# Three places for a group's transposes, and a residual added by VectorE behind the attention

## The chip, the cores and the metric

The kernel runs on one core of a Trainium2 chip. The metric is the device time of one execution in microseconds (us). TensorE (PE in the profile) does matmuls and writes PSUM; VectorE (DVE), ScalarE (ACT) and GpSimd (POOL) work on SBUF, the first two on PSUM as well; SyncE (SP) issues transfers, as POOL does for weights.

## The reference

Two branches over one normalised input, S = 2048 tokens of D = 640, H = 32 heads of 20, F = 1536:

```python
xn = _layernorm(x)
q, k, v = split(xn @ wqkv)                      # 32 heads of 20
# token s attends to s, s-2, ..., s-14 (W = 8, dilation 2), -1e9 where the index is negative
attn = softmax(einsum("bhsd,bhswd->bhsw", q, kg) * 20 ** -0.5)
s = einsum("bhsw,bhswd->bhsd", attn, vg) @ wo
g = silu(silu(xn @ w1) @ w2)
return x + s * g
```

All is float32. The kernel splits every matmul operand into a high and a low part and adds three products (high by high, low by high, high by low), so each product stands three times in PE's stream.

## The kernel before, in words

The tokens are worked on in four groups of 512 (`NG = 4`; two halves of the sequence by two parities), each as four tiles (`T = 4`) of 128 tokens. A group passes through two stages.

`qkv_phase` computes q, k and v in four quarters of eight heads. A quarter runs over five chunks (`DC`) of the 640 inputs and, in each, over the four tiles, three matmuls each (L706 to L708). Behind a quarter, ScalarE moves the sums out of PSUM (L490, L493, L496), SP issues copies that shift k and v by partitions (`halo`, L508), and VectorE gets the attention of the quarter: the scores (L531 product, L534 sum, L540 to L544), the softmax (L553 to L556) and the values (L563 product, L568 and L571 sums), which end in the tile `O`. VectorE falls behind PE, so the attention of a group goes on through the next stage and into the next group's.

`ffn_phase` runs over the twelve chunks of F. PE computes the w1 product of chunk f (L862 to L864) and then the w2 product of chunk f - 1 (L741, L743). ScalarE applies SiLU twice (L868 high part, L869 full), VectorE takes the low part (L870). The result, through SiLU, is the gate tile `G` (L901).

The attention's result must be turned before it meets `wo`. `o_chunk` does this for 128 columns of `O`: four transposes on PE into one of two PSUM banks `rot` (L474, in `split_t`), a copy by ScalarE (L478) and the low part by VectorE (L479). For groups 0 to 2 the five chunks are turned in the QKV stage of the next group, at places given by `O_AT` as (quarter, chunk). For the last group chunks 0 to 2 are turned in its own feed-forward stage (`OL_AT`), and chunks 3 and 4 together by `o_rest` (L589 transposes, L592 and L593 copies), two tiles at f = 11 and two at f = 12 (`REST_AT`).

`wo_phase` of group g stands behind the first w1 unit of group g + 1: five `wo` units, then VectorE multiplies the gate by each sum (L773), which also frees PE's accumulators for w2. Then it adds the residual: SP loads x into one of two tiles `XR` (L779), POOL adds (L780), SP stores (L782). An entry called "hold" keeps VectorE free for 3.4 us in the planned order. `wo_last` does the same for the last group at the end of the kernel, with VectorE adding the residual (L799, L801) and SP storing each part as it is done (L805).

Weights come through a ring of seven tiles `w`. In group 0 and in part in group 1 they are loaded raw by SP (L378), split by ScalarE (L406) and VectorE (L412), and the halves stored (L417); later they are loaded ready by POOL (L398). The raw loads of `wo` fall into group 1.

The order of instructions on each engine is made ahead of time. Each step is handed to `Weave.add` with its engine, an assumed duration, the keys that it reads and writes, and a priority. `Weave.order` plays these through and gives every engine a fixed order; PE keeps the order in which its steps were added. On the chip an engine works through its list and waits at an instruction until its inputs are ready, with everything behind it waiting too.

Of the kernel before, what the change touches and what calls it, by code (L numbers as in the profile page):

```python
# [14 lines left out]
P = 128  # L15
# [160 lines left out]
def local_attention_silu_ffn(ctx: ExitStack, tc: tile.TileContext, x, wqkv, wo, w1, w2, out):  # L176
# [52 lines left out]
    ACC = [psum.tile([P, TOK], F32, name=f"acc{i}") for i in range(6)]  # L229
    ROT = [psum.tile([P, TOK], F32, name=f"rot{i}") for i in range(2)]  # L230
    carry = [dram.tile([2, NQ, 2, T, CQ], F32, name=f"carry{par}") for par in range(2)]
    PRK = [("pr", k) for k in range(DC)]
    count = {"acc": 0, "rot": 0, "t": 0, "xr": 0}

# [101 lines left out]
    def raw_load(k):  # L336


        if k >= len(fresh):
            return  # L340
        i = fresh[k]
        u = units[i]
        n = width(i)
        if k < DC:
            r, kr = PR.rearrange("p t w m -> p (t w m)")[:, k * n:(k + 1) * n], [PRK[k]]
        elif k < early:
            s = (k - DC) % 6
            r, kr = (XR[s], [("xr", s)]) if s < 2 else (G[:, s - 2, :], [("g", s - 2, 0), ("g", s - 2, CA)])
            r = r[:, :n]
        else:  # L350
            s = k % 2
            r, kr = XR[s][:, :n], [("xr", s)]
        raws[i] = r, kr
        more = []
        if u[0] == "q":
            _, q, c = u
            cols, m, at = parts(i), 3, 0
            whole = wqkv[c * P:(c + 1) * P, :]
            src = whole.rearrange("p (s m) -> p s m", s=3)[:, :, q * CQ:(q + 1) * CQ]
            if i >= first_q:  # L360
                if q < NQ - 1:
                    odd, lies = cols[3], 3 * CQ
                else:
                    odd, lies, src, m, at = cols[0], 0, src[:, 1:], 2, cols[0][1]
                more.append((r[:, lies:lies + odd[1]], whole[:, odd[0]:odd[0] + odd[1]]))
            dst = r[:, at:at + m * CQ].rearrange("p (s m) -> p s m", s=m)
        elif u[0] == "w1":
            src = w1.rearrange("(c p) f -> p c f", p=P)[:, :, u[1] * P:(u[1] + 1) * P]
            dst = r.rearrange("p (c f) -> p c f", c=DC)
        else:  # L370
            m = wo if u[0] == "wo" else w2
            src, dst = m[u[1] * P:(u[1] + 1) * P, :], r
        if k in BY_ACT:
            add("ACT", 0.65, lambda: nc.scalar.dma_start(dst, src), [], kr, -1, nbytes=n * P * 4)
            return

        def go():
            nc.sync.dma_start(dst, src)  # L378
# [311 lines left out]
    def qkv_phase(g, i, io):  # L690
        for q in range(NQ):
            if g == 0 and q == 0:
                ps = first_quarter(i)
            else:
                ps = [bank() for t in range(T)]
                for c in range(DC):
                    wh, wl, kh, kl = w_next("q", q, c)
                    for t in range(T):
                        o, kp = ps[t]

                        n = wh.shape[-1]

                        def unit(c=c, t=t, o=o, wh=wh, wl=wl, n=n):
                            o = o[:, :n]
                            hi, lo = TH[i][:, c, tsl(t)], TL[i][:, c, tsl(t)]
                            nc.tensor.matmul(o, hi, wh, start=c == 0, stop=False)  # L706
                            nc.tensor.matmul(o, lo, wh, start=False, stop=False)  # L707
                            nc.tensor.matmul(o, hi, wl, start=False, stop=c == DC - 1)  # L708
# [50 lines left out]
    def wo_phase(g, i):  # L759
# [11 lines left out]
        for p, kp, ts, cs in tm_views(banks):  # L771
            n = (ts.stop - ts.start) * (cs.stop - cs.start)
            dve(n, lambda p=p, ts=ts, cs=cs: nc.vector.tensor_tensor(  # L773
                out=G[:, ts, cs], in0=p, in1=G[:, ts, cs], op=OP.mult), [kp], gkeys(ts, cs), 0)
        add("DVE", HOLD, lambda: None, [("g", t, CA) for t in range(T)], ["hold"], 0)
        for t in range(T):
            s = take("xr", 2)
# [3 lines left out]
                [("g", t, 0), ("g", t, CA)], [("xr", s)], 500, lock=True)  # L781
            dma(lambda t=t, xr=xr: nc.sync.dma_start(rows(og, g)[:, t, :], xr), [("xr", s)], [], P * D * 4, clock[0] + 20)  # L782

    def wo_last(g, i):

        banks = tm_banks()
# [4 lines left out]
        tk = t_keys(i, range(DC))  # L791
        xr = [XR[t] if t < 2 else XIN[:, t, :] for t in range(T)]
        kx = [("xr", t) if t < 2 else ("xin", t) for t in range(T)]
        for t in range(T):
            dma(lambda t=t: nc.sync.dma_start(xr[t], rows(xg, g)[:, t, :]), [], [kx[t]], P * D * 4, clock[0] - 20)

        def give(p, kp, t, cs):
            n = cs.stop - cs.start
            dve(n, lambda: nc.vector.tensor_tensor(out=G[:, t, cs], in0=p, in1=G[:, t, cs], op=OP.mult),  # L799
                [kp], [("g", t, cs.start)], 0)  # L800
            dve(n, lambda: nc.vector.tensor_tensor(out=xr[t][:, cs], in0=xr[t][:, cs], in1=G[:, t, cs], op=OP.add),  # L801
                [("g", t, cs.start)], [kx[t]], 0, lock=True)

        def leave(t, cs):
            dma(lambda: nc.sync.dma_start(rows(og, g)[:, t, cs], xr[t][:, cs]), [kx[t]], [], P * 4 * (cs.stop - cs.start), 0)  # L805

        def whole(t, cols):
            for k in range(3):
# [4 lines left out]
        A, B = slice(0, CA), slice(CA, D)  # L813
        for t in range(T - 1):
            pe(15 * TM, lambda t=t: whole(t, (0, 1)), tk + kw, [a[t][1], b[t // 2][1]])
            give(a[t][0][:, :CA], a[t][1], t, A)
            if t:
                for u in range(t // 2 * 2, t + 1):
                    give(b[t // 2][0][:, u % 2 * CB:(u % 2 + 1) * CB], b[t // 2][1], u, B)
                    leave(u, slice(0, D))  # L820
        t = T - 1
        pe(15 * mm(CA), lambda: whole(t, (0,)), tk + kw, [a[t][1]])
        give(a[t][0][:, :CA], a[t][1], t, A)
        leave(t, A)

        def rest():
# [4 lines left out]
        pe(15 * mm(CB), rest, tk + kw, [klast])  # L831
        give(lastb[:, :CB], klast, t, B)
        leave(t, B)

    def ffn_phase(g, i, ix, io):
        nxt = g + 1 if g + 1 < NG else None
        ps = prev = None
        for f in range(FC + 1):
# [15 lines left out]
            if f < FC:  # L854
# [1 line left out]
                h, kp = rot()  # L856
                s = f % 2

                def first(wh=wh, wl=wl, h=h):
                    for c in range(DC):  # L860
                        cs = tsl(c)
                        nc.tensor.matmul(h, wh[:, cs], TH[i][:, c, :], start=c == 0, stop=False)  # L862
                        nc.tensor.matmul(h, wh[:, cs], TL[i][:, c, :], start=False, stop=False)  # L863
                        nc.tensor.matmul(h, wl[:, cs], TH[i][:, c, :], start=False, stop=c == DC - 1)  # L864
                pe(15 * mm(TOK), first, t_keys(i, range(DC)) + [kh, kl], [kp])
# [77 lines left out]
```

## Time and profile before

| | |
|---|---|
| three runs | 639.21, 639.41, 638.80 us; median 639.21 |
| the profiled execution | 639.21 us, its span 637.4 us |
| granted TensorE clock | 0.999 |
| busy: PE / DVE / ACT / POOL | 630.3 / 536.9 / 211.3 / 122.5 us |
| HBM read, written | 109.55 MB, 34.16 MB |

Rows of a timeline give start and length in us from the start of the span, the engine (a q behind it is its queue: issues and waits), the source line, the operation, the output tile and the inputs, the shape, and in brackets how long the engine had been idle and who ended that. Matmuls overlap, so the distance from one start to the next is what one costs in a full stream, not its length. Lines of groups give count, total and mean. Lines of waits give who waited, for whom, the total in us, how often, and the longest.

### The profile page before, as it was taken

The numbers are of one execution on the slowest core, as the hardware profiler recorded it, in microseconds if no ns is written. First come the engines' busy times: TensorE is split into PE (matmuls) and PEld (weight loads), VectorE is DVE, ScalarE is ACT, GpSimd is POOL, SyncE is SP. The second block draws the span as 40 slices with busy tenths as digits, with TensorE's granted clock in tenths as the row PEclk, the third lists the DMA queues.
The fourth block names the chain that finished last, engine by engine and source line by source line (L and its number), as shares of the span: only waits on it lengthen the run. The fifth ranks groups of instructions, "written<-read, shape, count | busy, mean of one in ns | idle before, by whom it ended". The sixth has DMA issues, their size and how long they took to land.

```text
span 637.4 us, 9082 instructions
## 1 busy us (share of the span) xinstructions
PE 630.3 (99%) x3495; PEld 569.1 (89%) x3495; DVE 536.9 (84%) x539; ACT 211.3 (33%) x439; POOL 122.5 (19%) x168
## 2 busy tenths in 40 slices
PE   7999999999999999999999999999999999999997
PEld 6888899998889989999888999999988999899997
DVE  7699899999989799999969998998405997999844
ACT  5436453443435013142422402324313231131420
POOL 4500000001110133111222125212122213311100
PEclk9999999999999999999999999999999999999999
DMA  9999999876998999657699988865679999966522
GB/s 282 302 316 297 325 392 407 321 215 218 294 300 257 349 323 295 205 176 219 194 244 234 323 241 298 276 192 164 177 198 261 244 328 275 299 214 198 174 83 82
DMA packets 77499, 162.45 MB, mean 255 GB/s; under 512 B 9248, under 2 KB 38912, under 8 KB 77456
## 3 DMA queue, kind: packets, MB, share of 16 engines
q0 software_dynamic: 26672, 82.58, 44.1%
q1 hardware_dynamic: 50240, 78.88, 39.5%
q8 instruction: 27, 0.44, 0.3%
q10 hardware_dynamic: 544, 0.41, 0.2%
q14 instruction: 16, 0.13, 0.1%
HBM read 109.55 MB, written 34.16 MB: 225 GB/s over the span
## 4 chain that ended last, share of the span: by engine, by line
PE 92%; DVE 4%; DMA 3%; issue 1%; ACT 0%; DVEq 0%; ACTq 0%
PE acc L741 20%; PE acc L743 14%; PE acc L706 10%; PE acc L707 10%; PE acc L708 10%; PE rot L864 8%; PE rot L863 8%; PE rot L862 8%; DMA xr<-in_A_wo_dram 2%; PE rot L474 2%; PE acc L649 2%; DVE w L412 1%; DVE st L614 1%; DMA xin<-in_A_x_dram 0%; DVE gate L773 0%
## 5 line engine op out<-in xcount | busy, mean ns | idle before, releaser
L706 PE MATMUL acc<-w,th 128*128 128x512 f32 (+2 forms) x300 | 114.4, 381 | 0.0
L741 PE MATMUL acc<-w,sh 128*128 128x384 f32 x384 | 113.7, 335 | 0.0
L707 PE MATMUL acc<-w,tl 128*128 128x512 f32 (+2 forms) x300 | 113.1, 377 | 0.0
L708 PE MATMUL acc<-w,th 128*128 128x512 f32 (+2 forms) x300 | 112.9, 376 | 0.0
L743 PE MATMUL acc<-w,sh 128*128 128x256 f32 x384 | 107.2, 279 | 0.1
L531 DVE TENSOR_TENSOR pr<-q,kv 128x2560 f32<-128x2560 f32 x32 | 90.3, 2823 | 10.5 <-DMA kv<-kv 10.4
L862 PE MATMUL rot<-th,w 128*128 128x512 f32 x240 | 95.4, 398 | 0.0
L864 PE MATMUL rot<-th,w 128*128 128x512 f32 x240 | 94.1, 392 | 0.0
L863 PE MATMUL rot<-tl,w 128*128 128x512 f32 x240 | 93.9, 391 | 0.0
L563 DVE TENSOR_TENSOR pr<-e,kv 128x2560 f32<-128x2560 f32 x32 | 90.3, 2823 | 0.7
L534 DVE TENSOR_REDUCE l<-pr 128x128 f32<-128x2560 f32 x32 | 90.0, 2814 | 0.3
L398 POOL DMA_DIRECT2D w<-half_q x52 | 37.3, 717 | 239.3 <-DVE pr L568 93.2
L568 DVE TENSOR_TENSOR pr<-pr 128x1280 f32<-128x1280 f32 x64 | 79.1, 1235 | 1.1
L398 POOL DMA_DIRECT2D w<-half_w x72 | 38.7, 537 | 189.5 <-PE acc L743 84.5
L743 PEld LDWEIGHTS acc<-w,sh 128*128 128x128 f32 x384 | 72.3, 188 | 2.1 <-DVE gate L773 0.4
L741 PEld LDWEIGHTS acc<-w,sh 128*128 128x128 f32 x384 | 72.1, 188 | 1.7
L868 ACT ACTIVATE sh<-rot 128x512 fp32r<-128x512 f32 x48 | 28.7, 598 | 129.8 <-PE rot L864 129.7
L708 PEld LDWEIGHTS acc<-w,th 128*128 128x128 f32 x300 | 56.3, 188 | 9.0
L706 PEld LDWEIGHTS acc<-w,th 128*128 128x128 f32 x300 | 56.3, 188 | 8.6
L707 PEld LDWEIGHTS acc<-w,tl 128*128 128x128 f32 x300 | 56.4, 188 | 8.5
L741 PE MATMUL acc<-w,sl 128*128 128x384 f32 x192 | 57.8, 333 | 0.0
L864 PEld LDWEIGHTS rot<-th,w 128*128 128x128 f32 x240 | 45.0, 188 | 9.9
(93 smaller groups left out, 982.9 us busy)
## 6 DMA issues: line engine op xcount, KB each, us to landing
w<-half_w POOLq DMA_DIRECT2D x72, 640.0 KB, 5.4
w<-half_q POOLq DMA_DIRECT2D x39, 512.0 KB, 4.1
half_w<-w SPq DMA_DIRECT2D x24, 640.0 KB
w<-half_wo POOLq DMA_DIRECT2D x15, 640.0 KB, 8.4
kv<-kv SPq DMA_DIRECT2D x16, 560.0 KB
kv<-kv SPq DMA_DIRECT2D x16, 420.0 KB
gate<-in_B_w_dram SPq DMA_DIRECT2D x16, 320.0 KB
w<-half_q POOLq DMA_DIRECT2D x13, 384.0 KB, 5.4
```

The lines of the kernel that those rows point to most:

```text
L531: dve(2560, lambda t=t: nc.vector.tensor_tensor(out=PR, in0=win(qq[:, t:t + 2, :], W, 0), in1=win(kv[:, 0, t:t + 2, :], W, CQ), op=OP.mult ...
L534: dve(2560, lambda t=t: nc.vector.tensor_reduce(out=l[:, t:t + 2].rearrange("p t w h -> p (t w h)"), in_=PR.rearrange("p t w (h d) -> p (t ...
L563: dve(2560, lambda t=t, v=v: nc.vector.tensor_tensor(out=PR.rearrange("p t w (h d) -> p t (w h) d", d=DH), in0=e[:, t:t + 2].rearrange("p ...
L568: dve(2 * n * CQ, lambda n=n: nc.vector.tensor_tensor(out=PR[:, :, 0:n, :], in0=PR[:, :, 0:n, :], in1=PR[:, :, n:2 * n, :], op=OP.add), [] ...
L706: nc.tensor.matmul(o, hi, wh, start=c == 0, stop=False)
L707: nc.tensor.matmul(o, lo, wh, start=False, stop=False)
L708: nc.tensor.matmul(o, hi, wl, start=False, stop=c == DC - 1)
L741: nc.tensor.matmul(a[t][0][:, :CA], st, w[:, :CA], start=first, stop=last)
L743: nc.tensor.matmul(b[t // 2][0][:, h * CB:(h + 1) * CB], st, w[:, CA:], start=first and h == 0, stop=last, skip_group_check=True)
L862: nc.tensor.matmul(h, wh[:, cs], TH[i][:, c, :], start=c == 0, stop=False)
L863: nc.tensor.matmul(h, wh[:, cs], TL[i][:, c, :], start=False, stop=False)
L864: nc.tensor.matmul(h, wl[:, cs], TH[i][:, c, :], start=False, stop=c == DC - 1)
```

## The change

It does three things. The five chunks of `O` of groups 0 to 2 are turned at three places of the next group's QKV stage, each behind a whole quarter: chunks 0 and 1 behind quarter 1, chunks 2 and 3 behind quarter 2, chunk 4 behind quarter 3. The residual of group 2, whose gate is finished in the last group's feed-forward stage, is no longer added by POOL there, and the hold is not planned; `wo_rest` has VectorE add it when the last group's attention is done, with two of the four x tiles in `XR` and two in the tile `PR`, which the attention then no longer needs. The last group's second `o_rest` moves from f = 12 into the last w1 unit, between its twelfth and thirteenth matmul. The last group's own residual uses the four tiles of `XIN`, and its steps carry finer keys.

```diff
-    O_AT = {(1, 1): 0, (1, 4): 1, (2, 3): 2, (3, 1): 3, (3, 3): 4}
+    O_AT = {(1, 4): (0, 1), (2, 4): (2, 3), (3, 4): (4,)}
-    REST_AT = {11: (0, 1), 12: (2, 3)}
+    REST_AT = {11: (0, 1)}
...
                     if g and (q, c) in O_AT:
-                        o_chunk(g - 1, O_AT[q, c], io)
+                        for k in O_AT[q, c]:
+                            o_chunk(g - 1, k, io)
...
@@ wo_phase, behind the products by the gate
+        if g == NG - 2:
+            for t in range(T):
+                xr, kx = (XR[t], [("xr", t)]) if t < 2 else (PRV[:, (t - 2) * D:(t - 1) * D], PRK)
+                rest.append((t, xr, kx))
+                if t < 2:
+                    dma(lambda t=t, xr=xr: nc.sync.dma_start(xr, rows(xg, g)[:, t, :]), [], kx, P * D * 4, clock[0] + 5)
+            return
         add("DVE", HOLD, lambda: None, [("g", t, CA) for t in range(T)], ["hold"], 0)
...
+    def wo_rest(g):
+        done = [("o", NQ - 1, t) for t in (0, 2)]
+        for t, xr, kx in rest:
+            if t >= 2:
+                dma(lambda t=t, xr=xr: nc.sync.dma_start(xr, rows(xg, g)[:, t, :]), done, [(kx[0], t)] if t > 2 else kx,
+                    P * D * 4, clock[0])
+        for t, xr, kx in rest:
+            kx = [(kx[0], t)] if t > 2 else kx
+            dve(D, lambda t=t, xr=xr: nc.vector.tensor_tensor(out=xr, in0=xr, in1=G[:, t, :], op=OP.add),
+                done + gkeys(slice(t, t + 1), slice(0, CA)) + gkeys(slice(t, t + 1), slice(CA, D)), kx, 600, lock=True)
+            dma(lambda t=t, xr=xr: nc.sync.dma_start(rows(og, g)[:, t, :], xr), kx, [], P * D * 4, clock[0] + 5)
...
@@ wo_last
-        xr = [XR[t] if t < 2 else XIN[:, t, :] for t in range(T)]
+        xr = [XIN[:, t, :] for t in range(T)]
...
@@ ffn_phase, the w1 unit
+                if nxt is None and f == FC - 1:
+                    pe(12 * mm(TOK), lambda first=first: first(range(4)), t_keys(i, range(DC)) + [kh, kl], [kp])
+                    o_rest(g, (2, 3), io)
+                    wo_rest(g - 1)
+                    pe(3 * mm(TOK), lambda first=first: first(range(4, DC)), t_keys(i, range(DC)) + [kh, kl], [kp])
+                else:
+                    pe(15 * mm(TOK), first, t_keys(i, range(DC)) + [kh, kl], [kp])
```

More of the change, by code (lines that the diff above doesn't have):

```diff
@@ L790, in wo_last @@
         kw = [k for w in ws for k in w[2:]]
[L791 to L793 removed]
+        tk = lambda t: t_keys(i, range(DC), [t])
+        xr = [XIN[:, t, :] for t in range(T)]
+        A, B = slice(0, CA), slice(CA, D)
+        kx = lambda t, *cs: [("xin", t)] + [("xin", t, c.start) for c in cs]
         for t in range(T):
[L795 removed]
+            dma(lambda t=t: nc.sync.dma_start(xr[t], rows(xg, g)[:, t, :]), [], kx(t, A, B), P * D * 4, clock[0] - 20)
         def give(p, kp, t, cs):
@@ L801, in give, with leave @@
             dve(n, lambda: nc.vector.tensor_tensor(out=xr[t][:, cs], in0=xr[t][:, cs], in1=G[:, t, cs], op=OP.add),
-                [("g", t, cs.start)], [kx[t]], 0, lock=True)
-        def leave(t, cs):
-            dma(lambda: nc.sync.dma_start(rows(og, g)[:, t, cs], xr[t][:, cs]), [kx[t]], [], P * 4 * (cs.stop - cs.start), 0)
+                [("g", t, cs.start)], kx(t, cs)[1:], 0, lock=True)
+        def leave(t, *cs):
+            at = slice(cs[0].start, cs[-1].stop)
+            dma(lambda: nc.sync.dma_start(rows(og, g)[:, t, at], xr[t][:, at]), kx(t, *cs)[1:], [],
+                P * 4 * (at.stop - at.start), 0)
         def whole(t, cols):
@@ L857, in ffn_phase, with first @@
                 s = f % 2
-                def first(wh=wh, wl=wl, h=h):
-                    for c in range(DC):
+                def first(cs=range(DC), wh=wh, wl=wl, h=h):
+                    for c in cs:
                         cs = tsl(c)
```

16 lines of the change are left out of this document (8 added, 8 removed).

## The prediction

> **What bounds the kernel now.** I read the page first: busy shares, then the chain that ended last.
>
> ```profile
> PE 630.3 (99%) x3495; PEld 569.1 (89%) x3495; DVE 536.9 (84%) x539; ACT 211.3 (33%) x439; POOL 122.5 (19%) x168
> ...
> PE 92%; DVE 4%; DMA 3%; issue 1%; ACT 0%; DVEq 0%; ACTq 0%
> ```
>
> TensorE (PE) is busy for 630.3 of 637.4 us and makes up 92% of the chain. A busy share can hide stalls, so next came the view of who waited for whom, for PE's rows and its weight loads (total us, times, longest).
>
> ```profile
> PE rot L628 <- DVE xin L619: 1.6, 3, 0.8
> PE rot L602 <- POOL ident masks.py:199: 1.4, 1, 1.4
> PE acc L649 <- DVE tl L636: 0.3, 1, 0.3
> ...
> PEld acc L743 <- DVE gate L773: 0.4, 1, 0.4
> ```
>
> The first three lie in the first quarter, at the start of the program, which the change leaves alone. The last is the only stall of the matmul stream behind it. So the change can gain on the path only what it takes out of PE's own stream, plus that 0.4 us, and it can lose by any new wait of PE. 0.2% of the time, about what a measurement of this kernel can tell from no change, is 1.28 us.
>
> **Part 1, transposes in three places instead of five.** In groups 1 to 3 PE still turns five chunks of O, with the same 60 transposes. The edit removes two breaks of the matmul stream in each group. Cost of a break, from PE's timeline (start, length) and the row of that line (min/median/max ns):
>
> ```profile
> 166.55 0.39 PE L708 MATMUL acc<-w,th 128*128 128x512 f32 x1
> 166.78 0.60 PE L474 MATMUL rot<-ident,o 128*128 128x128 f32 x4
> 167.13 0.49 PE L706 MATMUL acc<-w,th 128*128 128x512 f32 x1
> 167.46 0.39 PE L707 MATMUL acc<-w,tl 128*128 128x512 f32 x1
> ...
> L474 PE MATMUL rot<-ident,o x72: 270/272/273, 166.8 to 597.4; 128*128 128x128 f32 x72
> ```
>
> From the transposes' start to the second matmul behind them are 0.68 us; one matmul's spacing (166.55 to 166.78) is 0.23, so four transposes cost the stream 0.45 us. Four starts fit into 0.60 - 0.27 = 0.33 us, so the spacing is 0.11 and four of them are 0.44. Being a break of its own costs therefore only about 0.02 us, and 2 x 3 merged breaks give 6 x 0.02 = 0.1 us. Bounds, since no row shows eight transposes in a row: 0 if the second four wait for their bank as they do now, 6 x 0.45 = 2.7 if they vanished in the pipeline. I take 0.1, which the spacing of rows gives.
>
> Moving them shifts data dependencies too. Chunk 3 is turned two weight chunks earlier than now, behind quarter 2. It needs the O of quarter 3 of the group before. In group 1, where VectorE is fullest, its timeline has the last write of it here, and ScalarE's last eviction of quarter 2, which follows that quarter's matmuls, stands below it:
>
> ```profile
> 183.76 0.49 DVE L571 TENSOR_TENSOR o<-pr 128x320 f32<-128x320 f32 x1
> ```
> ```profile
> 190.24 0.44 ACT L490 ACTIVATE kv<-acc 128x320 f32<-128x320 f32 x1
> ```
>
> O is there 6 us before the turn: no wait.
>
> **Part 2, group 1, where VectorE's order changes.** The written order of the changed kernel puts the score reduction L534 ahead of the last `wo` weight's low half (L412), where now it is behind. The rows of VectorE, and of PE where it stalls:
>
> ```profile
> 217.58 0.83 DVE L412 TENSOR_TENSOR w<-xr,w 128x640 fp32r<-128x640 f32 x1 [3.93 <-ACT w L406]
> 218.32 2.81 DVE L534 TENSOR_REDUCE l<-pr 128x128 f32<-128x2560 f32 x1
> 221.17 2.83 DVE L563 TENSOR_TENSOR pr<-e,kv 128x2560 f32<-128x2560 f32 x1
> 223.91 3.14 DVE L773 TENSOR_TENSOR gate<-acc,gate 128x384 f32<-128x384 f32 x6
> ```
> ```profile
> 226.66 0.33 PE L741 MATMUL acc<-w,sh 128*128 128x384 f32 x1
> 227.11 0.39 PE L743 MATMUL acc<-w,sh 128*128 128x256 f32 x1
> ```
>
> VectorE idles 3.93 us for that weight and then has L534, L563 and the six L773 that free PE's accumulators. 227.11 - 226.66 is 0.45 where such a pair is 0.17 apart, and the following step is also 0.1 longer: 0.38 us lost. With L534 in the 3.93 us hole, L563 and L773 come 2.8 us earlier and the loss goes: -0.38.
>
> The same weight can become the next wait. PE first needs its low half at 218.89, and VectorE ends it at 218.41. Its raw load stands in SP's queue behind the halo copies of quarter 3, and those wait for ScalarE's last eviction L490. In the new order chunk 4's eviction L478 stands ahead of that L490:
>
> ```profile
> 167.41 0.60 ACT L478 ACTIVATE th<-rot 128x512 fp32r<-128x512 f32 x1 [0.51 <-PE rot L474]
> ...
> 201.59 0.44 ACT L490 ACTIVATE kv<-acc 128x320 f32<-128x320 f32 x1
> ...
> 216.81 0.74 ACT L406 ACTIVATE w<-xr 128x640 fp32r<-128x640 f32 x1 [10.68 <-DMA xr<-in_A_wo_dram]
> ```
> ```profile
> 202.05 4.50 SPq L508 DMA_DIRECT2D kv<-kv  x4
> ...
> 207.41 0.36 SPq L378 DMA_DIRECT2D xr<-in_A_wo_dram  x1
> ```
> ```profile
> 201.39 0.39 PE L862 MATMUL rot<-th,w 128*128 128x512 f32 x1
> ...
> 218.89 0.33 PE L741 MATMUL acc<-w,th 128*128 128x384 f32 x1
> ```
>
> The quarter's stream ends at 201.39 in either order, so chunk 4 is turned from 201.39 - 0.45 = 200.9; L478 follows 0.63 us behind the start of a turn (166.78 to 167.41) and takes up to 0.60, so L490 starts at 202.1 instead of 201.59. Halo copies, raw load (207.41) and L412 move by the same 0.5 us if the transfer does: end at 218.9 against a need at 218.86. Loss 0.05; between 0 (the transfer hides the shift) and 0.5 (the transfer, 9.4 us from 207.41 to 216.81, is longer by 0.5 as well).
>
> **Part 3, the other residual in the last group.** In group 3 four POOL adds leave, VectorE's planned hold goes, and behind the attention VectorE gets four adds of 640 columns, SP two loads into `pr` (the other two, into `xr`, come early) and four stores. One row of the waits of VectorE between 534 and 637, and its timeline:
>
> ```profile
> DVE sl L870 <- ACT sf L869: 7.6, 6, 4.0
> ```
> ```profile
> 550.53 4.09 DVE L568 TENSOR_TENSOR pr<-pr 128x1280 f32<-128x1280 f32 x2
> ...
> 602.59 0.69 DVE L870 TENSOR_TENSOR sl<-sf,sh 128x512 fp32r<-128x512 f32 x1 [1.32 <-ACT sf L869]
> 603.20 0.48 DVE L571 TENSOR_TENSOR o<-pr 128x320 f32<-128x320 f32 x1
> 603.72 2.83 DVE L563 TENSOR_TENSOR pr<-e,kv 128x2560 f32<-128x2560 f32 x1
> ...
> 607.06 2.34 DVE L568 TENSOR_TENSOR pr<-pr 128x1280 f32<-128x1280 f32 x2
> ```
>
> In the new order the last L571, which completes O, stands right behind the L870 of 602.59. So 0.5 + 2.8 + 2.3 = 5.6 us of work must come ahead of it. There are 7.6 us of waits, the longest the hold's, and 4.09 - 2.34 = 1.7 us that L568 lost beside a POOL add: 9.3 us of room. O is then complete at 603.7. PE turns its last half inside the last w1 unit, behind 12 of 15 matmuls:
>
> ```profile
> 607.34 0.39 PE L864 MATMUL rot<-th,w 128*128 128x512 f32 x1
> ...
> 611.70 0.60 PE L589 MATMUL rot<-ident,o 128*128 128x128 f32 x4
> ...
> 612.74 0.34 PE L741 MATMUL acc<-w,sl 128*128 128x384 f32 x1
> ```
>
> That is at 607.6, 3.9 us later than O. The turn itself moves (from 611.70) and adds nothing. What is queued behind the new adds on VectorE is the split of both halves of O and the last L870, for which PE's matmul of 612.74 waits. The two adds out of `xr` (0.83 each, as L412) end at 605.4; the two out of `pr` wait for loads issued from 603.8 on:
>
> ```profile
> 539.56 1.58 SPq L779 DMA_DIRECT2D xr<-in_A_x_dram  x2
> ```
> ```profile
> 545.45 1.59 POOL L780 TENSOR_TENSOR xr<-xr,gate 128x640 f32<-128x640 f32 x1
> ```
>
> The first of two loads of this size, issued at 539.56, was in use by POOL at 545.45: it took at most 5.9 us, so 609.7 here, and the second, 0.8 us (half of 1.58) behind it, is there when the first add is done. Two adds, the second split and L870 (1.6 + 0.6 + 0.6) then end at 612.5, 0.2 us before the need. Cost 0, with that cover. Behind the matmuls the chain is unchanged: last eviction, add, store.
>
> **Sum.** The profiled execution is 639.21 us (span 637.4 and 1.8 around it), which is also the median. -0.1 - 0.38 + 0.05 = -0.43: 638.8, a span of 637.0. With the bounds of these terms it is 638.3 to 639.3, and the three runs scatter by 0.6.
>
> **Rivals.** (a) Slower: the loads into `pr` land late, VectorE holds L870 and PE stalls. For it: the load of 207.41 took 9.4 us in a busy stretch (216.81), and stores and weight loads run beside these too. Against: the rows around 540. It decides from 6.1 us of landing on (609.9); at 9.4 us PE loses 3.3: 642.1. At 7.9 us it passes 0.2%. (b) Slower: the last `wo` weight is late. Its load waits for the slot of the last w1 unit, which now ends 0.45 us later, beside 6 transfers of 320 KB.
>
> ```profile
> 608.71 0.53 POOL L398 DMA_DIRECT2D w<-half_wo  x1 [3.34 <-PE rot L864]
> ```
> ```profile
> w<-half_wo POOLq DMA_DIRECT2D x15, 640.0 KB, 8.4
> ```
> ```profile
> 616.94 0.34 PE L741 MATMUL acc<-w,th 128*128 128x384 f32 x1
> ```
>
> PE needs it at 616.94. The median of 8.4 us behind 609.2 gives 617.6, a loss of 0.7 (639.5); with another 2 us of contention it is 641.5. Against: the median is that of busier stretches, and this load made 616.94 without a stall. The Trainium skill ("DMA: Bandwidth & Descriptors", Queues, rings and completion order) says that a DMA engine serves its queues in turn, packet by packet; by that the weights would share with the stores and not stand behind all of them. No run here shows it for this pair yet. The skill also has a rule against the change ("SBUF — State Buffer", SBUF: two separate sides): VectorE can lock the port over which POOL writes its descriptors. By it the issue at 608.71 would slip by up to two adds, 1.7 us. The L398 rows do not show it: 0.53 us at 608.71, beside a running L568. (c) Faster: merged transposes cost almost nothing, 2.7 instead of 0.1 us: 636.2. Against: spacing 0.11 within four. (d) Faster: VectorE, not PE, sets the end, and the 5.6 us of work done sooner show: 633.2. Against: PE's list of waits has no such row. (e) The `wo` weight of group 1 stalls by the full 0.5: 639.2, still within 0.2%.
>
> **How the numbers follow.** Forecast 638.8 with 0.72, (e) 0.06, (a) 0.09, (b) 0.05, (c) 0.06, (d) 0.02. Within 0.2% are the forecast and (e), 0.78; slower (a) and (b), 0.14; faster (c) and (d), 0.08. 638.0 to 640.4 holds the forecast with the scatter of the runs, (e), and the mild ends of (a) and (b).
>
> **What would show it.** Right: PE's waits lose L743 <- L773 and gain nothing; eight transposes take about 0.89 us of stream; VectorE's last L571 lies near 603, and L870 still ends before PE's sl matmuls. Wrong: PE or its weight loads waiting at L741 of the fifth `wo` unit in group 1 (near 218.8), at L741 <- L870 near 612.7, or at the fifth `wo` weight near 617.

## The result, and the profile after

The changed kernel takes 642.74 us (median of 15 runs, 638.40 to 644.41) against 638.91 for the kernel before (15 runs, 638.70 to 640.68): 1.0042 times the time of before, with a 95% interval of 1.0026 to 1.0057. It is slower by 2.7 us by the ratio, and it scatters: the fastest run is below every run of before, the slowest 6 us above that. The mean granted clock tells the runs apart: seven runs between 638.40 and 641.19 have 0.999 or 1.000, and all eight from 642.74 up have 0.995 to 0.997. The traces shown below have the clock at half in stretches of 3.41 us; one such stretch takes 3.41 x 0.5 = 1.7 us of 640 from the mean clock, or 0.0027, so a run at 0.997 had one and a run at 0.995 two.

The profiled execution of the changed kernel took 643.34 us, its span is 641.5 and its clock 0.995. Source lines are one to four higher than in the kernel before around here (L406, L412, L741, L743, L773 are now L407, L413, L743, L745, L775). First the view of who waited for whom, PE's rows.

```profile
PE rot L629 <- DVE xin L620: 2.0, 3, 1.1
PE acc L743 <- ACT w L407: 1.5, 1, 1.5
PE rot L603 <- POOL ident masks.py:199: 1.4, 1, 1.4
PE acc L743 <- DVE w L413: 0.3, 1, 0.3
```

The stall by the gated multiply is gone, as forecast. Two waits are new, both for the fifth `wo` unit in group 1: PE waits for the high half of the weight (L407), then for the low half (L413). This is the first place that the prediction named as what would prove it wrong. PE's timeline there (start, length, line; in brackets the idle time and who ended it):

```profile
219.42 0.28 PE L745 MATMUL acc<-w,tl 128*128 128x256 f32 x1
221.18 0.45 PE L743 MATMUL acc<-w,th 128*128 128x384 f32 x1 [1.48 <-ACT w L407]
221.46 0.28 PE L745 MATMUL acc<-w,th 128*128 128x256 f32 x1
222.03 0.45 PE L743 MATMUL acc<-w,th 128*128 128x384 f32 x1 [0.30 <-DVE w L413]
...
222.78 0.53 PE L743 MATMUL acc<-w,th 128*128 128x384 f32 x1
223.10 0.41 PE L745 MATMUL acc<-w,th 128*128 128x256 f32 x1
...
225.99 0.38 PE L743 MATMUL acc<-w,th 128*128 128x384 f32 x1
```

A step of the full stream is 0.17 behind an L743 and 0.12 behind an L745. From 219.42 to 221.18 are 1.76 us, so 1.64 are lost; from 221.46 to 222.03 another 0.46. Then comes a second loss that is no wait: from 222.78 to 225.99 twelve matmuls take 3.21 us where six pairs take 1.71, with PE never idle. The windows view says why (columns: busy time of PE, its weight loads, VectorE, ScalarE, GpSimd, then granted clock, DMA share, GB/s):

```profile
218.00:221.50 3.50, 2.02 (x14) 1.74 (x13) 0.34 (x1) 0.74 (x1) 0.00 (x0) 1.00 1.06 408
221.50:226.00 4.50, 4.20 (x19) 3.97 (x18) 4.50 (x5) 0.00 (x0) 1.06 (x2) 0.63 0.89 297
226.00:232.00 6.00, 6.00 (x34) 5.41 (x34) 2.23 (x5) 1.09 (x2) 2.67 (x3) 1.00 0.76 274
```

The clock is at half behind the wait, for 3.41 us from 222.64 on. With 0.2 us at the edges of that stretch the place costs 1.64 + 0.46 + 1.50 + 0.23 = 3.8 us.

Why the weight came late, from the timelines of SP's queue, ScalarE and VectorE:

```profile
203.48 4.26 SPq L509 DMA_DIRECT2D kv<-kv  x4
...
208.31 0.36 SPq L379 DMA_DIRECT2D xr<-in_A_wo_dram  x1
```
```profile
202.53 0.60 ACT L479 ACTIVATE th<-rot 128x512 fp32r<-128x512 f32 x1 [0.41 <-PE rot L475]
203.03 0.43 ACT L491 ACTIVATE kv<-acc 128x320 f32<-128x320 f32 x1
...
220.38 0.74 ACT L407 ACTIVATE w<-xr 128x640 fp32r<-128x640 f32 x1 [12.85 <-DMA xr<-in_A_wo_dram]
```
```profile
221.16 0.83 DVE L413 TENSOR_TENSOR w<-xr,w 128x640 fp32r<-128x640 f32 x1 [4.22 <-ACT w L407]
```

This execution's PE is 0.93 us behind that of before at this point (1.15 from the start-up, less 0.22 gained by merged turns). So the load's issue, 208.31, is 207.38 in the time of before (with those 0.93 us taken off), against 207.41: not late, although the last eviction (202.10 against 201.59) and the halo copies (202.55 against 202.05) did move by the 0.5 us that was forecast. What is longer is the time of the transfer, 12.1 us from 208.31 until ScalarE can use it, against 9.4.

The first QKV matmul of groups 1, 2 and 3, in the kernel before and then in the changed one, cuts the difference of the two spans, 641.5 - 637.4 = 4.1 us, into parts:

```profile
147.69 0.40 PE L706 MATMUL acc<-w,th 128*128 128x512 f32 x1
...
303.92 0.40 PE L706 MATMUL acc<-w,th 128*128 128x512 f32 x1
...
459.74 0.40 PE L706 MATMUL acc<-w,th 128*128 128x512 f32 x1
```
```profile
148.84 0.40 PE L707 MATMUL acc<-w,th 128*128 128x512 f32 x1
...
308.34 0.40 PE L707 MATMUL acc<-w,th 128*128 128x512 f32 x1
...
463.95 0.40 PE L707 MATMUL acc<-w,th 128*128 128x512 f32 x1
```

Start-up +1.15, group 1 159.50 against 156.23 or +3.27, group 2 155.61 against 155.82 or -0.21, the rest -0.1. Group 1 is 3.8 of late weight, less the 0.4 of the old stall and the 0.2 of merged turns.

The start-up lies ahead of everything that the change touches, and with it goes a clock at half as well. PE's own windows (busy time of PE, granted clock, DMA share, GB/s) show the two stretches of this execution, and the window ahead of the second:

```profile
7.60:11.01 3.41, 3.41 (x12) 0.50 1.08 337
...
219.22:222.64 3.42, 1.64 (x10) 1.00 0.89 345
222.64:226.05 3.41, 3.41 (x15) 0.50 1.00 323
```

The profiled execution of the kernel before has no such stretch at its start. So 1.15 of the 4.1 us between these two profiles is not the work of the change. The mean clock of a run without a trace tells that a stretch was lost, not where: of 35 runs of the kernel before on the chip of the first experiments, four have 0.994 to 0.997 too, and take 640.49 to 642.30 us.

### The profile page after: what moved, and what is told of

The parts are those of the page before. It is cut to its first block, busy times and chain, and to the rows that moved or that the text cites. A ratio compares the mean times of both kernels' runs of the same rounds, so it can differ in the third digit from the quotient of the medians.

```text
span 641.5 us, 9077 instructions
## 1 busy us (share of the span) xinstructions
PE 632.7 (99%) x3495; PEld 572.1 (89%) x3495; DVE 537.5 (84%) x543; ACT 210.2 (33%) x439; POOL 117.7 (18%) x164
## 4 chain that ended last, share of the span: by engine, by line
PE 93%; DVE 3%; DMA 2%; issue 1%; ACT 0%; DVEq 0%; ACTq 0%
PE acc L743 21%; PE acc L745 14%; PE acc L709 9%; PE acc L707 9%; PE acc L708 9%; PE rot L890 8%; PE rot L889 8%; PE rot L888 8%; PE rot L475 2%; DMA xr<-in_A_wo_dram 2%; PE acc L650 2%; DVE w L413 1%; DMA xin<-in_A_x_dram 1%; DVE l L535 0%; DVE st L615 0%
## 5 line engine op out<-in xcount | busy, mean ns | idle before, releaser
L743 PE MATMUL acc<-w,sh 128*128 128x384 f32 x384 | 113.6, 335 | 0.0
L745 PE MATMUL acc<-w,sh 128*128 128x256 f32 x384 | 107.1, 279 | 0.0
L535 DVE TENSOR_REDUCE l<-pr 128x128 f32<-128x2560 f32 x32 | 90.1, 2815 | 0.4
L569 DVE TENSOR_TENSOR pr<-pr 128x1280 f32<-128x1280 f32 x64 | 76.0, 1188 | 1.0
L745 PEld LDWEIGHTS acc<-w,sh 128*128 128x128 f32 x384 | 72.3, 188 | 1.6
L743 PEld LDWEIGHTS acc<-w,sh 128*128 128x128 f32 x384 | 72.1, 188 | 1.7
L743 PE MATMUL acc<-w,sl 128*128 128x384 f32 x192 | 57.9, 333 | 0.0
L491 ACT ACTIVATE kv<-acc 128x320 f32<-128x320 f32 x64 | 28.3, 442 | 84.8 <-PE acc L709 82.2
```

What stands on the lines that cost most here:

```text
L535: dve(2560, lambda t=t: nc.vector.tensor_reduce(out=l[:, t:t + 2].rearrange("p t w h -> p (t w h)"), in_=PR.rearrange("p t w (h d) -> p (t ...
L743: nc.tensor.matmul(a[t][0][:, :CA], st, w[:, :CA], start=first, stop=last)
L745: nc.tensor.matmul(b[t // 2][0][:, h * CB:(h + 1) * CB], st, w[:, CA:], start=first and h == 0, stop=last, skip_group_check=True)
```

## Experiments

Theory: the late raw load of the last `wo` unit in group 1, with the fall of the clock behind it, is the whole loss, and it follows from where the chunks are turned. Rivals: the residual in the last group costs it; or the long runs are a matter of the chip and not of the kernel. Times beside each other below come from the same chip.

**The two halves of the change, and two repairs** (before: 639.08 us).

Places only, on the kernel before:

```diff
-    O_AT = {(1, 1): 0, (1, 4): 1, (2, 3): 2, (3, 1): 3, (3, 3): 4}
+    O_AT = {(1, 4): (0, 1), (2, 4): (2, 3), (3, 4): (4,)}
```

> Only the three places for the transposes; the residual stays with POOL and the hold stays. Theory A (the last wo weight's raw load comes late in group 1, through SP's queue and the places; the clock falls behind the stall): like the changed kernel, median 641 to 643.5, single runs from 638.3 to 644.5, a granted clock below 1 in the runs above 642, PE waiting near 219 us for ScalarE L406 or VectorE L412. Theory B (the residual part, through the order it gives VectorE and SP, is what costs): 638.2 to 638.6, no wait of PE at the fifth wo unit.

Measured: 640.42 us, 638.30 to 645.08 in twelve runs, ratio 1.0020 (1.0002 to 1.0038), the three runs at 641.94, 642.32 and 645.08 with a clock of 0.995 to 0.997. The places alone bring the whole spread. The median lies between the two forecasts, below the 641 of theory A: three of twelve runs lost clock here and eight of fifteen with the whole change, too few to tell whether the residual adds to it. The profiled run was the fastest and had no wait: its raw load, issued at 207.78, was in use at 214.60.

Residual only, the changed kernel with the old places:

```diff
-    O_AT = {(1, 4): (0, 1), (2, 4): (2, 3), (3, 4): (4,)}
+    O_AT = {(1, 1): (0,), (1, 4): (1,), (2, 3): (2,), (3, 1): (3,), (3, 3): (4,)}
```

> The residual part alone (VectorE's adds, no hold, the last turn inside the last w1 unit); the transposes at their five places. Theory A: 638.9, as before, the 0.4 us stall at L773 still there and all three groups 0.2 us longer on PE than in the changed kernel. Theory B: 641 to 643.5 with PE waiting at the fifth wo unit.

Measured: 639.24 us, 638.96 to 640.98, ratio 1.0004 (0.9996 to 1.0013): no difference. The residual is not the loss; its three longest runs (640.18, 640.93 and 640.98, at 0.997) are like the four of the kernel before. Its matmuls at the three stage starts:

```profile
147.69 0.40 PE L707 MATMUL acc<-w,th 128*128 128x512 f32 x1
...
303.51 0.40 PE L707 MATMUL acc<-w,th 128*128 128x512 f32 x1
...
459.34 0.40 PE L707 MATMUL acc<-w,th 128*128 128x512 f32 x1
```

Group 1 is 155.82, 0.41 shorter than before, and group 2 is unchanged (155.83 against 155.82). The old stall is gone, against theory A, but not by VectorE's order, which is here still that of the kernel before (the low half of the weight, L413, ahead of the reduction, L535):

```profile
215.71 0.83 DVE L413 TENSOR_TENSOR w<-xr,w 128x640 fp32r<-128x640 f32 x1 [2.07 <-ACT w L407]
216.46 2.81 DVE L535 TENSOR_REDUCE l<-pr 128x128 f32<-128x2560 f32 x1
```

The weight came sooner: ScalarE had it at 214.94 instead of 216.81, and with it everything behind it on VectorE. That is the scatter of one load (7.7 us from its issue at 207.21, against 9.4), in a stretch whose order is that of before.

Chunk 4 alone put back to where it is turned in the kernel before:

```diff
-    O_AT = {(1, 4): (0, 1), (2, 4): (2, 3), (3, 4): (4,)}
+    O_AT = {(1, 4): (0, 1), (2, 4): (2, 3), (3, 3): (4,)}
```

> The changed kernel with chunk 4 turned one weight chunk earlier, ahead of quarter 3's last chunk, so that ScalarE's last eviction of quarter 3 is not behind chunk 4's copy and the halo copies are issued some 0.5 to 0.9 us sooner. Theory A with chunk 4's place as the cause: 638.2 to 638.6, clock 1 in every run. Theory A with the place behind quarter 2 as the cause (two copies ahead of its last eviction, all of SP's queue 1.3 us later): still 640 to 643, stalls at the fifth wo unit in many runs. Theory B: 641 to 643.5.

Measured: 640.46 us, 639.38 to 641.24, ratio 1.0016 (1.0007 to 1.0025). Its list of waits still has the late weight:

```profile
PE acc L743 <- ACT w L407: 1.0, 1, 1.0
...
PE acc L743 <- DVE w L413: 0.3, 1, 0.3
```

So chunk 4, on which the prediction's step rested, is not by itself what makes the weight late, though with it back no run of eleven is longer than 641.24.

A buffer of its own for the raw load, which then goes out ahead of quarter 3's halo copies, and not when one of two `XR` tiles is free:

```diff
+    RAW = sb.tile([P, D], F32, name="rawlast")
...
-            r, kr = XR[s][:, :n], [("xr", s)]
+            r, kr = (RAW[:, :n], [("raw", 0)]) if units[i] == ("wo", DC - 1) else (XR[s][:, :n], [("xr", s)])
```

> The changed kernel with a buffer of its own for the raw load of the last wo weight, so that its load stands in SP's queue ahead of quarter 3's halo copies and needs no earlier split to end. Theory A: the stall and the fall of the clock go, 638.2 to 638.5, span some 4 us below the profiled changed kernel, no run with a clock below 0.999. Theory B: 641 to 643.5.

Measured: 638.43 us, and eleven runs lie within 638.22 to 638.60, all at a clock of 0.999 or more; ratio 0.9986 (0.9978 to 0.9995). It beats both kernels, and the long runs are gone with the wait. ScalarE has the weight 19 us ahead of need, and the group starts show what the rest of the change is worth:

```profile
198.96 0.74 ACT L408 ACTIVATE w<-rawlast 128x640 fp32r<-128x640 f32 x1 [5.38 <-PE acc L709]
```
```profile
147.97 0.40 PE L708 MATMUL acc<-w,th 128*128 128x512 f32 x1
...
303.57 0.40 PE L708 MATMUL acc<-w,th 128*128 128x512 f32 x1
...
459.18 0.40 PE L708 MATMUL acc<-w,th 128*128 128x512 f32 x1
```

Group 1 155.60 (-0.63 against before), group 2 155.61 (-0.21). The changed kernel's group 1 is longer than this by 159.50 - 155.60 = 3.9 us, the 3.8 counted above. With chunk 4 put back, where the profile has the wait and no low clock, it is longer by 1.9 (305.59 - 148.09 = 157.50): the wait without the clock.

**Later turns, a busy PE, the buffer without the change, made stalls** (another chip, before: 638.97 us).

The turns one weight chunk later, so that ScalarE's copies of the turned columns don't stand ahead of a quarter's last evictions:

```diff
-    O_AT = {(1, 4): (0, 1), (2, 4): (2, 3), (3, 4): (4,)}
+    O_AT = {(2, 0): (0, 1), (3, 0): (2, 3)}
...
                 if g and f == 0:
+                    o_chunk(g - 1, 4, io)
```

> The changed kernel with its three places moved one weight chunk later: chunks 0 and 1 turn behind the first weight chunk of quarter 2, chunks 2 and 3 behind the first weight chunk of quarter 3, chunk 4 behind the first matmuls of the feed-forward stage, so that ScalarE's copies of the turned columns no longer stand ahead of the last evictions of a quarter. Theory A (the copies of chunks 2 and 3 stand ahead of quarter 2's last eviction, so its halo copies and the stores ahead of the last wo raw load end later in SP's queue): the wait of TensorE for the fifth wo unit in group 1 goes or falls under 0.5 us, the clock stays at 0.998 or above, and the time is 638.0 to 638.8. Theory B (the late load follows from two turns standing at one place, wherever it is): the wait stays at 1 us or more and the time stays at 640 to 643.

Measured: 997.96 us. It says nothing on either theory. `PE rot L475 <- DVE o L572` is waited for 18 times, 334.7 us in all: turned this late, a chunk comes behind the next group's attention, whose O it then turns, so this is another computation. It does tell that the new places have less than one weight chunk to spare.

Eight matmuls on PE ahead of the fifth `wo` unit, to keep it busy through the wait (a first try):

```diff
+            if g == 0 and c == DC - 1:
...
+                    for n in range(8):
+                        nc.tensor.matmul(ROT[ri][:, :CA], OH[i][:, c - 1, tsl(0)], ph[:, :CA], start=True, stop=True)
...
```

> The changed kernel with eight matmuls of 384 columns into a free bank added on TensorE ahead of the fifth wo unit of group 1, whose result is not used: TensorE works through most of the wait. The theory that the wait itself costs at most 1.5 to 2.1 us and that the rest of the loss is the clock that falls to half after it: time 639.8 to 641.5, the clock at 0.998 or above in every run, the windows from 221 to 227 at full clock. The rival that the low clock is a matter of the chip and comes without a cause in the kernel: some runs again at 0.995 to 0.997 and above 642.5.

Measured: 654.15 us. The matmuls read `ph`, the fourth unit's weight, whose ring tile has by then been given to the next load, and PE waits 11.2 us for that load. The experiment failed by its own operand.

The own buffer alone, on the kernel before:

```diff
+    RAW = sb.tile([P, D], F32, name="rawlast")
...
+            r, kr = (RAW[:, :n], [("raw", 0)]) if units[i] == ("wo", DC - 1) else (XR[s][:, :n], [("xr", s)])
```

> The kernel before with a buffer of its own for the raw load of the fifth wo unit, so that the load goes out before the queue work of quarter 3. It shows what the rest of the change is worth without the late load: the changed kernel with this buffer ran in 638.43. If the rest of the change gains by the stall at the gated multiply and by the merged turns, 0.4 and 0.3 to 0.65: 638.8 to 639.4 here. If the own buffer itself were the gain of that version: 638.3 to 638.5 here, with little scatter.

Measured: 638.84 us, ratio 0.9999 (0.9990 to 1.0008). The buffer by itself is no gain that can be told; with the change it was 0.9986 (on another chip, against its own kernel before). So the change is a small gain where the weight is not late.

Six stalls of PE of rising length made on purpose in group 2's feed-forward stage, by a chain of ScalarE copies between two transposes:

```diff
+    STALL = {1: 0, 2: 1, 4: 2, 6: 3, 8: 4, 10: 6}
...
+            if g == 2 and f in STALL:
+                pe(0.11, lambda ri=ri: nc.tensor.transpose(ROT[ri][:, :P], ident, ident), [], [("rot", ri)])
...
+                for n in range(STALL[f]):
+                    act(TOK, lambda a=a, b=b: nc.scalar.activation(IDLE[b][:, :], IDLE[a][:, :], AF.Copy), [("idle", a)], [("idle", b)], 0)
...
+                pe(0.11, lambda ri=ri, z=z: nc.tensor.transpose(ROT[ri][:, :P], IDLE[z][:, :P], ident), [("idle", z)], [("rot", ri)])
```

> The kernel before with six made stalls of TensorE in group 2's feed-forward stage, of rising length: at its second, third, fifth, seventh, ninth and eleventh block TensorE waits for a chain of one short ScalarE copy and 0, 1, 2, 3, 4 or 6 copies of 512 columns, some 0.5 to 4.5 us. Theory (a wait of 1.5 us is enough for the clock to fall to half for some 3.4 us): behind the stalls of 0.5 us the matmuls stay at 0.22 us, behind those of 1.5 us or more they run at 0.43 us for some 3 us. Rival (the clock falls only behind an idle time of 3 us or more, and something else slowed the matmuls of the changed kernel): doubled spacing behind the last one or two stalls alone.

Measured, from one matmul's start to the next: 0.6, 1.4, 2.0, 2.6, 3.7 and 5.0 us. Neither expectation holds. The clock falls behind 2.6 and 5.0 and not behind 3.7, as the windows just behind the third, fourth, fifth and sixth show (columns as in the first table of windows):

```profile
403.10:408.00 4.90, 4.88 (x25) 4.27 (x26) 4.83 (x5) 3.51 (x5) 0.53 (x1) 1.00 0.78 283
...
419.70:424.50 4.80, 4.80 (x15) 3.83 (x16) 4.01 (x2) 0.00 (x0) 0.00 (x0) 0.65 0.25 91
...
440.00:444.00 4.00, 4.00 (x19) 3.36 (x20) 2.27 (x4) 3.12 (x4) 0.00 (x0) 1.00 0.00 0
...
459.80:464.00 4.20, 4.20 (x11) 3.33 (x12) 0.00 (x0) 0.00 (x0) 0.00 (x0) 0.50 0.00 0
```

**The changed kernel again, a mended PE filler, an earlier turn, equal stalls** (a third chip, before: 638.94 us, 638.43 to 639.79).

The changed kernel itself:

> The changed kernel unchanged, on the chip of the next two runs. Theory (the late load and the clock): its times spread from 638.4 to 644.4 again, those above 642 all with a clock below 0.998, and the profile shows TensorE waiting for the fifth wo unit in group 1 by 0.5 to 2.5 us. Rival (one chip's whim): all times between 638.3 and 640 and no such wait.

Measured: 642.46 us, 640.02 to 645.19 in nine runs, ratio 1.0050 (1.0032 to 1.0068); five runs above 642 at a clock of 0.995 to 0.997, four below 641.2 at 0.999 or more. Its profile has the same two waits, 1.7 and 0.3 us, and again a clock of 0.62 from 221.5 to 226. It is not one chip's whim.

The filler again, reading the O of group 0 instead of a weight:

```diff
+            if g == 0 and c == DC - 1:
...
+                    for n in range(8):
+                        nc.tensor.matmul(ROT[ri][:, :CA], OH[i][:, c - 1, tsl(0)], OH[i][:, 0, :CA], start=True, stop=True)
...
```

> The changed kernel with eight matmuls of 384 columns into a free bank ahead of the fifth wo unit of group 1, their result unused, and every other instruction of every engine in the same order as in the changed kernel (in the first try with such matmuls GpSimd's adds and weight loads changed places, which cost 11 us). They take 8 x 0.165 = 1.3 us, which a run without the wait pays in full. Theory (the wait is 1.5 to 2.1 us, the rest of the loss is the clock that falls behind it): all runs between 639.7 and 641.5 with the clock at 0.998 or above, so a slowest run some 3 us below that of the changed kernel. Rival (the low clock has no cause in this wait): runs above 642.5 with a clock of 0.995 to 0.997 as often as in the changed kernel.

Measured: 641.13 us, ratio 1.0039 (1.0026 to 1.0052): 639.68, 640.55, 641.13, 641.52 at 0.999 or more, and one run at 642.77 with 0.997. (The text on record puts the 11 us of the first try down to GpSimd's order; PE's wait of 11.2 us for the operand accounts for them.) The floor moved up by the 1.3 us of filler, from 638.4 to 639.7, and four of five runs stay within the forecast; the fifth does not. Five runs are too few to tell how much of the spread the filler takes away: it leans to the theory and settles nothing.

Chunks 2 and 3 one weight chunk earlier, still two at once and three places:

```diff
-    O_AT = {(1, 4): (0, 1), (2, 4): (2, 3), (3, 4): (4,)}
+    O_AT = {(1, 4): (0, 1), (2, 3): (2, 3), (3, 4): (4,)}
```

> The changed kernel with chunks 2 and 3 turned one weight chunk earlier, behind the fourth chunk of quarter 2 and not behind its end; still two at once, still three places. ScalarE's and VectorE's work on the turned columns then ends ahead of the last eviction of quarter 2. Theory (that work stands ahead of the last eviction, so halo copies, the stores of the wo halves and the last raw load end later in SP's queue): no wait of TensorE for the fifth wo unit in group 1 over 0.4 us, clock at 0.998 or above, time 638.2 to 638.9, as with a buffer of its own for that load. Rival (what makes the load late is that it is a long transfer, 12 and not 9.3 us, whatever stands ahead): wait and spread stay as in the changed kernel, 640 to 643.

Measured: 638.85 us, ratio 1.0005 (0.9994 to 1.0016) against 1.0050 for the changed kernel beside it; one of eleven runs (642.46) has the low clock. In its profile no wait for the weight is left:

```profile
207.12 0.36 SPq L379 DMA_DIRECT2D xr<-in_A_wo_dram  x1
```
```profile
217.18 0.74 ACT L407 ACTIVATE w<-xr 128x640 fp32r<-128x640 f32 x1 [10.69 <-DMA xr<-in_A_wo_dram]
```

So it is the turn of chunks 2 and 3 behind quarter 2's last matmuls that makes the load late more often. The load was issued at 207.1 to 208.3 in every profile that shares a tile for it. From there until ScalarE had it were, in the six with that turn, 6.8 (places only), 9.8 (second filler), 11.7 (first filler), 11.8 (changed, again), 11.9 (chunk 4 back) and 12.1 us (changed); in the five without it 7.7 (residual only), 8.0 (six stalls), 8.6 (twelve stalls, below), 9.4 (before) and 10.1 (here). The stated reason is not shown. The turn does move the queue ahead: the raw loads of the third and fourth unit leave SP about a microsecond later. But the fastest load of all, 6.8, has that too. The length of the transfer decides, it differs between runs of one order of instructions, and what makes it long more often in the changed order stays open. The DMA engines are fully busy in that stretch in both kernels (a share of 1.10 and 1.05 from 205 to 218).

Twelve stalls of equal make in group 2 (the line differs from the kernel with six):

```diff
-    STALL = {1: 0, 2: 1, 4: 2, 6: 3, 8: 4, 10: 6}
+    STALL = {f: 2 for f in range(1, 13)}
```

> The kernel before with twelve made stalls of TensorE of the same length, 1.96 us by the earlier run with rising steps (there the matmuls fell to half pace behind 2.6 and 5.0 us, and not behind 1.4, 2.0 and 3.7 us). Theory (what counts is how much of a fixed window, running on by itself, is idle, so that the same stall lowers the clock or not by where it falls): some of the twelve are followed by 3 to 4 us of matmuls at 0.43 us and some are not. Rival 1 (a fixed length of idle time decides): all twelve alike. Rival 2 (the late load's stall of 2.1 us was not what lowered the clock): none of the twelve.

Measured: seven of 1.96 to 2.02 us from start to start, and five of 2.34. None of the seven was followed by a lower clock; of the five, two were. Equal stalls, unequal clocks: the length of the idle time alone does not decide.

The traces show what does. Wherever one of them has more than one low stretch, their starts lie whole multiples of 3.413 us apart: 436.46 and 446.70 here (3 times), 421.17 and 458.72 with the six stalls (11 times), 7.60 and 222.64 in the changed kernel (63 times). So the clock is set in windows of 3.41 us that run on through the whole execution. Cut into these windows, two of the five stalls of 2.34 us lie whole in one; the first two lines are the first of them and the window behind it. The next two are a third stall, cut in half by a boundary, and the last two the stall of 3.7 us of the run before (PE's own windows, columns as above):

```profile
433.05:436.46 3.41, 1.34 (x8) 1.00 0.60 193
436.46:439.88 3.42, 3.42 (x10) 0.50 0.01 2
...
453.53:456.95 3.42, 2.38 (x18) 1.00 0.56 186
456.95:460.36 3.41, 2.38 (x11) 1.00 0.56 191
```
```profile
434.83:438.24 3.41, 1.70 (x14) 1.00 0.64 191
438.24:441.65 3.41, 1.73 (x8) 1.00 0.40 149
```

Inside the executions of all fourteen traces, every full-clock window in which PE was busy for 1.48 us or less was followed by one at half clock (15 windows), and none with 1.66 us or more was (over 2500). Of the three windows between, 1.57 was not followed by one, 1.63 and 1.64 were; the ends of matmuls are modelled, so the border is not known more finely. The 1.64 is the changed kernel's: its wait, 1.64 and 0.46 us lost, lies whole in the window from 219.22 to 222.64. By these numbers a boundary in the midst of it would have spared the clock. This fits the runs of the changed kernel that lose only the wait (up to 641.2) and those that lose the clock as well (from 642.5); for runs without a trace it is not shown.

## Why the prediction was wrong, point by point

**What bounds the kernel** was right: only a new wait of PE could cost, and that is what came.

**Part 1, the merged turns.** Mis-sized, on the safe side: 0.1 us forecast, 0.63 found (0.21 in each of three groups, 0.10 for each break saved). Eight transposes at once cost the stream 0.88 us (from PE's starts), as forecast with 0.89. A single turn in quarters 1 and 2 costs more than the 0.45 counted: the ten matmuls that follow it start 0.231 apart on average and not 0.227, another 0.04 that the two rows behind the turn did not show. Behind the eight transposes of quarter 1 only two matmuls are slower.

**Part 2, the stall that goes.** The mechanism was right, the size was that of one execution. In the run with chunks 2 and 3 turned earlier, VectorE has the changed order, and although ScalarE had its weight later than before (at 217.18 against 216.81), it reaches the gated multiplies 2.5 us sooner (221.43 against 223.91) and PE has no stall:

```profile
213.18 2.82 DVE L535 TENSOR_REDUCE l<-pr 128x128 f32<-128x2560 f32 x1
217.95 0.83 DVE L413 TENSOR_TENSOR w<-xr,w 128x640 fp32r<-128x640 f32 x1 [1.95 <-ACT w L407]
...
221.43 3.14 DVE L775 TENSOR_TENSOR gate<-acc,gate 128x384 f32<-128x384 f32 x6
```

But four profiles have the old order in group 1, and only the one in which the load took 9.4 us has the stall; at 7.7, 8.0 and 8.6 us (residual alone, six and twelve stalls) it is absent and group 1 is 155.8 us. So 0.38 was a gain only against that one execution, and came from the same row, taken for a constant, as the next step.

**Part 2, the last `wo` weight.** Here the prediction failed, in its bound. It named the wait and the place, followed the shift of the issue, and took 0.05 us with at most 0.5, "the transfer ... is longer by 0.5 as well". The last eviction and the halo copies moved as forecast, but the load's issue did not; the transfer took 12.1 us instead of 9.4. The 9.4 was one row of one execution, in a stretch of fully busy DMA engines, and it was used as if it were a constant; the runs show 6.8 to 12.1. With a need only 0.5 us behind the end of the weight's split this term's bound should have been the scatter of transfers, not the shift of an issue. Rival (e), the full 0.5 for 639.2, was the right wait at a quarter of its size: 2.1 us. The chunk blamed was the wrong one too: chunk 4 put back leaves the wait, chunks 2 and 3 moved remove it.

**Left out of the sum altogether:** what a wait of PE does to its clock. The sum counted idle time only. Behind 2.1 us of it came 1.7 us more at half clock, so that the term forecast as 0.05, at most 0.5, measured 3.8. The Trainium skill has a page on it ("TensorE: Matmul & The Clock Gate", Part 1: The HAM clock gate): the clock is gated to half by activity in a window of some 3.4 us that runs on by itself. The traces agree with the half clock, with the 3.41 us that it lasted and with a window that runs on by itself (starts 3, 11 and 63 windows apart). The same page's rule of no idle gaps over about 3.4 us (HAM oscillation) does not hold here: two of five stalls of 2.34 us were enough, and one of 3.7, cut by a boundary, was not.

**Part 3, the residual in the last group.** Right about the waits: PE has none by the new adds, although VectorE waits 1.95 us for the loads into `pr`. VectorE's timeline in the changed kernel, all of it some 4 us later by the loss in group 1:

```profile
606.89 0.49 DVE L572 TENSOR_TENSOR o<-pr 128x320 f32<-128x320 f32 x1
607.30 1.55 DVE L804 TENSOR_TENSOR xr<-xr,gate 128x640 f32<-128x640 f32 x2
...
612.27 1.56 DVE L804 TENSOR_TENSOR pr<-pr,gate 128x640 f32<-128x640 f32 x2 [1.95 <-DMA pr<-in_A_x_dram]
...
614.35 0.68 DVE L902 TENSOR_TENSOR sl<-sf,sh 128x512 fp32r<-128x512 f32 x1
```

O was complete at 607.4, 603.4 in the time of before against 603.7 forecast, and the last L902 ended at 615.03, 1.8 us ahead of PE's product by that `sl` (616.88). The forecast cover was 0.2; the loads, in use 4.9 us after their issue (607.41 to 612.27), were a microsecond quicker than the 5.9 assumed. "Moves and adds nothing" was off by 0.15: PE's starts from the last w1 unit on show that the turn between its twelfth and thirteenth matmul costs that much more than between the units of before.

**Rivals.** (a) loads into `pr`, (b) the last `wo` weight at the end and (d) did not come. For (b): that weight's issue stands at 613.16, 609.2 in the time of before as forecast, and takes 0.53 us with an add of VectorE running beside it, so nothing slipped. Of (c), 2.7 us for merged transposes that cost almost nothing, 0.63 came.

Without the late weight the time would have been in the range: 638.8 predicted, 638.43 with the own buffer. That is in part luck: the gain that its trace shows is 0.63 us of merged turns, less 0.15 at the end, and not 0.1 of turns and 0.38 of stall.

## What to carry to other kernels

A weight that is ready 0.5 us ahead of its need, behind a load in a stretch of fully busy DMA engines, is not covered: price it by the spread of such transfers over several executions, and give it a buffer that lets it go out early before anything around it is moved. A wait of TensorE over some 2 us may cost nearly as much again in clock, and not in every run, so read the windows behind a wait, and read a kernel's scatter beside its clock before believing one profile. A profile that disagrees with another can also differ where the change does nothing, as at the start here: cut the difference into parts before explaining it. The version to keep here is the changed kernel with the raw load's own buffer: 638.43 us, faster than both and with a scatter of 0.4 us.

## What the hardware showed that was not expected

- TensorE's clock is set for windows of 3.41 us that run on through the execution. Behind a window in which PE was busy for 1.48 us or less it was at half every time, behind one with 1.66 us or more never. So none of eight stalls of 1.96 to 2.02 us cost clock, two of five of 2.34 us did, and one of 3.7 us, cut by a boundary, did not.
- The same 320 KB load, at the same place in its queue, took 6.8 to 12.1 us until its first use, over eleven profiles.
- Transposes that break into a stream of matmuls slow the ten matmuls behind four of them by 0.04 us in all (at a spacing of 0.227), and only two behind eight.
